# An attention block and a gated feed-forward network on one core: feed-forward chunks of 510 tokens across batches, outputs accumulated in four banks

## Chip, cores and metric

One core of a Trainium2 chip runs the whole kernel. The metric is device microseconds (us) of one execution; lower is better. The engines are PE (matrix products; PEld is its loading of the stationary operand), DVE (VectorE), ACT (ScalarE), POOL (GpSimd) and SP, which issues the DMAs. Tiles have 128 partitions; PSUM, where PE writes, has eight banks of 512 float32 each per partition.

## What is computed

Eight batches, eight heads of 64, 512 local tokens and 32 global ones per batch. Local tokens attend to the 32 global ones and to local ones up to 32 away; global tokens attend to all. The 544 rows of a batch (global first) are the input `x` (512 wide) of a gated network with a convolution of three taps along the tokens of a batch:

```python
out_g = np.matmul(sm(s_g), v_all)                       # 32 global queries, all keys
s_ll = np.where(mask, s_ll, -1000000000.0)              # |i - j| <= 32
out_l = np.matmul(sm(np.concatenate([s_lg, s_ll], axis=-1)), np.concatenate([v_g, v_l], axis=2))
...
h = np.maximum(x @ w_in, 0.0)                           # 512 -> 1024
for k in range(K):                                      # K = 3, zeros at a batch's two ends
    conv_out += conv_w[k][None, None, :] * hp[:, k:k + S, :]
gate = 1.0 / (1.0 + np.exp(-conv_out))
return (h * gate @ w_out).astype(np.float32)            # 1024 -> 512
```

`w_in`, `conv_w` and `w_out` arrive as float64; everything else is float32.

## The kernel before

**Layout.** Features lie on partitions and tokens run along the free dimension. To keep precision, each factor of the two network products is split in a high and a low part of a reduced float32 type, and a product is three matmuls: high by high, high by low, low by high.

**Weights.** Eight packs of 128 × 1024 float64 (four of `w_in`, four of `w_out`) are loaded as pairs of 32-bit words by WD (L171) and decoded: absolute value on ACT (WA, L112), clamp, shift and join of the sign on DVE (WC: L119, L120, L123), the high part cast on ACT (WH, L212), and the low part on DVE from the power of two and the remaining bits (WL: L126, L130, L132, L134). One tile `wt` serves all packs in turn; the raw tiles share their space with the tiles of `g`.

**Attention**, by pair of heads: scores (SC, L264), mask and maximum on DVE (MA, L285), exponentials with their sum on ACT (EX, L295), transposes (TR, L304) copied back by ACT (AT, L212), the product with the values (PV, L325), division (NO, L333), a transpose (UP, L341), then the high part XH (ACT) and the low part XL (DVE, L364) of `x`. The global tokens, four heads at a time, go through G (L278), GM, GE, GT (L406), GC, GP (L422), GO, GQ (L436) and GX, which writes their columns of `x`.

**Network.** A unit is one of 16 half batches (272 tokens) and one of eight feature tiles `ft`. Z (L460) makes twelve matmuls of 274 columns, the half batch and a neighbour on either side, into a bank `ps_h`. RE (L469, ACT) applies the maximum into one of two lasting tiles `hb` whose ends are zero. C1 (L248, POOL) is the middle tap; Ca and Cb (L484, DVE) add the outer ones. For two feature tiles at a time, 544 wide, follow TH (tanh, L493, ACT), GG (the gate times h, L498, DVE), GH (high part, ACT) and GL (low part, L215, on POOL in the first batch, on DVE later). O (L523) is done per half batch and output tile `mt`: two parts Oa and Ob, each of four feature tiles and twelve matmuls of 272 columns, into one bank `ps_o`; OE (L212, DVE) copies it out and ST stores it.

**Order.** `plan` and `units` list all these steps with what they need and which tiles or banks they take. `arranged` simulates them with the costs of `cost` and the limits `SLOTS` and `LIMIT`; among the steps that are ready on an engine, one with the lowest position goes first, and positions come from tables of numbers (`POS0` for the first batch, `POS` for later ones, `WPOS` for weight packs, `LATE`). `emit` issues the steps in that order, and each engine executes its own in exactly that order, whatever is ready.

Of the kernel before, what the change touches and what calls it, by code (L numbers as in the profile page):

```python
# [52 lines left out]
def attn_moe(ctx: ExitStack, tc: tile.TileContext, qk_d, vw_d, qg_d, w_in_d, w_out_d, cw_d, out_d):  # L53
# [61 lines left out]

    def scaled_bits(w1, t, keep):

        v = nc.vector
        v.tensor_scalar(out=f(t), in0=f(t), scalar1=LEAST, scalar2=MOST, op0=ALU.max, op1=ALU.min)  # L119
        v.tensor_scalar(  # L120
            out=t, in0=t, scalar1=3, scalar2=0x3F800000 | keep, op0=ALU.logical_shift_left, op1=ALU.bitwise_and
        )
        v.scalar_tensor_tensor(out=t, in0=w1, scalar=0xC0000000, in1=t, op0=ALU.bitwise_and, op1=ALU.bitwise_or)  # L123
# [4 lines left out]
    def rest(on, out, w0, w1, p, low):  # L128

        nc.vector.tensor_scalar(out=w1, in0=w1, scalar1=low, scalar2=None, op0=ALU.bitwise_and)  # L130
# [1 line left out]
        v.scalar_tensor_tensor(out=f(w1), in0=w0, scalar=2.0**-32, in1=w1, op0=ALU.mult, op1=ALU.add)  # L132
        if on == "v":
            v.scalar_tensor_tensor(out=out, in0=f(w1), scalar=2.0**-20, in1=f(p), op0=ALU.mult, op1=ALU.mult)  # L134
# [210 lines left out]
    def x_of(b, ct, half):  # L345
        if (b, ct, half) not in xs:
            xs[b, ct, half] = (xp.tile([P, HW], F32R, name="xh"), xp.tile([P, HW], F32R, name="xl"))
        return xs[b, ct, half]

    def outputs(n, half):  # L350
# [2 lines left out]
        xh, xl = x_of(b, h // 2, half)
        if half == 0:
            return heads[n]["pv"][:, 0 : HW - SG], xh[:, SG:HW], xl[:, SG:HW]
        return heads[n]["pv"][:, SL - HW : SL], xh, xl

    def XH(n, half):
        pv, xh, xl = outputs(n, half)
        cp("XH", xh, pv)  # L360

    def XL(n, half):
        pv, xh, xl = outputs(n, half)
        nc.vector.tensor_tensor(out=xl, in0=pv, in1=f(xh), op=ALU.subtract)  # L364
# [86 lines left out]
    def Z(u):  # L451
        hh, ft = divmod(u, NFT)
        b, half = divmod(hh, 2)
        st = hid[u] = {"h": hb[u // 2 % SLOTS["hb"]][:, u % 2, half : half + HW]}
        ps = st["z"] = bank([P, HW], "ps_h")
        i = 0
        for ct in range(NCT):
            xh, xl = x_of(b, ct, half)
            for w, x in ((w_in[0], xh), (w_in[0], xl), (w_in[1], xh)):
                nc.tensor.matmul(ps, lhsT=w[:, ft, ct, :], rhs=x, start=i == 0, stop=i == 3 * NCT - 1)  # L460
# [11 lines left out]

    def C1(u):
        st, ft = hid[u], u % NFT
        if u % 2 == 0:
            st["two"] = moe.tile([P, 2, HALF], F32, name="t", bufs=SLOTS["t"])
        else:
            st["two"] = hid[u - 1]["two"]
        st["t"] = st["two"][:, u % 2, :]
# [441 lines left out]
```

## Time and profile before

| | |
|---|---|
| median of three runs | 595.39 us (595.06 to 596.19) |
| profiled execution, device time | 595.32 us |
| its span in the trace | 593.5 us |
| mean granted TensorE clock | 0.982 |
| ACT busy | 324.2 us (55%) |
| DMA | 68.46 MB, mean 115 GB/s |

The page gives busy time by engine over the whole span; the trace is then asked for stretches of time (windows), for the chain of work that ended last, and for groups of like instructions. In 40 slices of 14.8 us the busy tenths of PE and the granted clock are:

```profile
PE   5656997999999999999999999999999999999997
DVE  4999999689477948577685858668584856565651
POOL 6000242033012111121111012111101212221210
PEclk9977999899999999999999999999999999999999
```

The first seven slices differ from all others: PE is half busy there, DVE at nine tenths, POOL free for three of them.

### The profile page before, as it was taken

The numbers are of one execution on the slowest core, as the hardware profiler recorded it, in microseconds if no ns is written. First come the engines' busy times: TensorE is split into PE (matmuls) and PEld (weight loads), VectorE is DVE, ScalarE is ACT, GpSimd is POOL, SyncE is SP. The second block draws the span as 40 slices with busy tenths as digits, with TensorE's granted clock in tenths as the row PEclk, the third lists the DMA queues.
The fourth block names the chain that finished last, engine by engine and source line by source line (L and its number), as shares of the span: only waits on it lengthen the run. The fifth ranks groups of instructions, "written<-read, shape, count | busy, mean of one in ns | idle before, by whom it ended". The sixth has DMA issues, their size and how long they took to land.

```text
span 593.5 us, 20757 instructions
## 1 busy us (share of the span) xinstructions
PE 560.9 (95%) x8704; PEld 528.8 (89%) x8704; DVE 424.0 (71%) x1388; ACT 324.2 (55%) x994; POOL 101.1 (17%) x190
## 2 busy tenths in 40 slices
PE   5656997999999999999999999999999999999997
PEld 3345896999999999999999999999999999999997
DVE  4999999689477948577685858668584856565651
ACT  4954794676477666446565655555565543333320
POOL 6000242033012111121111012111101212221210
PEclk9977999899999999999999999999999999999999
DMA  6987334156234332123333222232412000000001
GB/s 254 390 286 313 95 118 170 39 204 223 91 135 153 107 134 98 56 110 108 135 108 145 100 78 94 100 144 97 146 63 75 20 22 20 29 20 29 30 29 47
DMA packets 22125, 68.46 MB, mean 115 GB/s; under 512 B 2576, under 2 KB 12816, under 8 KB 21008
## 3 DMA queue, kind: packets, MB, share of 16 engines
q1 hardware_dynamic: 22032, 67.14, 31.2%
q8 instruction: 68, 1.11, 0.8%
q14 instruction: 25, 0.20, 0.1%
HBM read 58.22 MB, written 8.91 MB: 113 GB/s over the span
## 4 chain that ended last, share of the span: by engine, by line
PE 84%; DVE 9%; ACT 2%; issue 1%; DMA 1%; POOL 0%; DVEq 0%
PE ps_o L523 32%; PE ps_h L460 31%; PE ps_v L325 5%; PE ps_s L264 4%; PE ps_t L304 4%; PE pv L341 2%; PE psg L278 2%; PE go L422 2%; PE gt L406 1%; DVE pr L285 1%; DVE t L484 1%; DMA vf<-vw 1%; DVE wt L123 1%; DVE raw L132 1%; ACT pr L295 1%
## 5 line engine op out<-in xcount | busy, mean ns | idle before, releaser
L460 PE MATMUL ps_h<-xh,w_in 128*128 128x274 f32 x1024 | 225.4, 298 | 2.8 <-DVE raw L132 1.3
L523 PE MATMUL ps_o<-g,w_out 128*128 128x272 f32 x1536 | 212.2, 290 | 0.0
L523 PEld LDWEIGHTS ps_o<-g,w_out 128*128 128x128 f32 x1536 | 200.0, 189 | 0.2
L460 PEld LDWEIGHTS ps_h<-xh,w_in 128*128 128x128 f32 x1024 | 171.9, 191 | 6.3 <-ACT g L212 1.4
L248 POOL TENSOR_SCALAR t<-hb,cw 128x272 f32<-128x272 f32 x128 | 79.9, 629 | 425.7 <-ACT hb L469 159.2
L460 PE MATMUL ps_h<-xl,w_in 128*128 128x274 f32 x512 | 149.5, 292 | 0.8 <-issue 0.8
L484 DVE SCALAR_TENSOR_TENSOR t<-hb,cw,t 128x272 f32<-128x272 f32 x256 | 125.7, 514 | 30.5 <-POOL t L248 29.1
L295 ACT ACTIVATE pr<-pr,negm 128x128 f32<-128x128 f32 x256 | 99.5, 391 | 47.7 <-DVE negm L285 47.7
L469 ACT ACTIVATE hb<-ps_h 128x273 f32<-128x273 f32 x128 | 50.8, 398 | 93.4 <-PE ps_h L460 91.9
L460 PEld LDWEIGHTS ps_h<-xl,w_in 128*128 128x128 f32 x512 | 98.1, 192 | 1.0 <-issue 1.0
L285 DVE CUSTOM_DVE_ANT_0 pr<-ps_s,mask 128x128 f32<-128x128 f32 x256 | 57.8, 285 | 25.6 <-PE ps_s L264 23.2
L212 DVE COPY o<-ps_o 128x272 f32<-128x272 f32 x64 | 28.0, 438 | 54.8 <-PE ps_o L523 54.6
L212 ACT CAST g<-t 128x544 fp32r<-128x544 f32 x64 | 40.9, 646 | 34.5 <-DVE t L498 22.6
L498 DVE SCALAR_TENSOR_TENSOR t<-t,hb 128x544 f32<-128x544 f32 x64 | 46.0, 719 | 14.3 <-ACT t L493 13.3
L493 ACT ACTIVATE t<-t 128x544 f32<-128x544 f32 x64 | 42.4, 663 | 15.0 <-DVE t L484 13.9
L212 ACT COPY a<-ps_t 128x512 f32<-128x512 f32 x64 | 37.0, 583 | 23.2 <-PE ps_t L304 23.0
L295 ACT ACTIVATION_READ_ACCUMULATOR pr<-pr,negm 128x1 f32 x256 | 48.3, 189 | 0.0
L264 PE MATMUL ps_s<-qk 64*32 64x128 f32 x2048 | 38.4, 283 | 8.4 <-DMA qk<-qk 5.8
L304 PE MATMUL ps_t<-ident,pr 128*128 128x128 f32 x256 | 43.0, 282 | 3.5 <-ACT pr L295 2.5
L215 DVE TENSOR_TENSOR g<-t,g 128x544 fp32r<-128x544 f32 x56 | 41.0, 737 | 6.8 <-ACT g L212 5.3
L264 PEld LDWEIGHTS ps_s<-qk 64*32 64x32 f32 x2048 | 29.9, 109 | 12.7 <-DMA qk<-qk 5.8
L304 PEld LDWEIGHTS ps_t<-ident,pr 128*128 128x128 f32 x256 | 31.1, 144 | 8.2 <-ACT pr L295 7.6
(70 smaller groups left out, 466.1 us busy)
## 6 DMA issues: line engine op xcount, KB each, us to landing
vf<-vw SPq DMA_DIRECT2D x32, 896.0 KB, 6.3
qk<-qk SPq DMA_DIRECT2D x32, 592.0 KB, 4.9
out<-o SPq DMA_DIRECT2D x64, 136.0 KB, 1.7
raw<-w_in SPq DMA_DIRECT2D x4, 1024.0 KB, 6.6
raw<-w_out SPq DMA_DIRECT2D x4, 1024.0 KB, 6.6
qgf<-qg SPq DMA_DIRECT2D x16, 64.0 KB, 2.0
cwr<-cw SPq DMA_DIRECT2D x1, 24.0 KB, 1.9
```

Of the source, the lines that this page charges most:

```text
L212: nc.scalar.copy(out=out, in_=in_) if choice(key) == "a" else eng(key).tensor_copy(out=out, in_=in_)
L248: nc.gpsimd.tensor_scalar(out=out, in0=in_, scalar1=by, scalar2=0.0, op0=ALU.mult, op1=ALU.add)
L264: nc.tensor.matmul(heads[n + j]["s"][b * SG : (b + 1) * SG, t, :], lhsT=qk[rows, i * SG : (i + 1) * SG], rhs=qk[rows, a : a + P], start=Tr ...
L285: nc.vector.tensor_tensor_reduce(out=pr[:, t, :], in0=st["s"][:, t, :], in1=mask[:, t].rearrange("p a c -> p (a c)"), op0=ALU.add, op1=ALU ...
L295: nc.scalar.activation(out=st["p"][:, t, :], in_=st["p"][:, t, :], func=AF.Exp, scale=-1.0, bias=st["m"][:, t : t + 1], accum_out=two["r"] ...
L304: nc.tensor.transpose(out=st["t"][:, t, :], in_=st["p"][:, t, :], identity=ident)
L460: nc.tensor.matmul(ps, lhsT=w[:, ft, ct, :], rhs=x, start=i == 0, stop=i == 3 * NCT - 1)
L469: nc.scalar.activation(out=o, in_=z, func=AF.Relu, scale=0.5)
L484: nc.vector.scalar_tensor_tensor(out=st["t"], in0=st["h"][:, k : k + HALF], scalar=cw[:, 3 * ft + k : 3 * ft + k + 1], in1=st["t"], op0=AL ...
L493: nc.scalar.activation(out=t, in_=t, func=AF.Tanh)
L498: nc.vector.scalar_tensor_tensor(out=t, in0=t, scalar=1.0, in1=h, op0=ALU.add, op1=ALU.mult)
L523: nc.tensor.matmul(ps, lhsT=w[:, mt, ft, :], rhs=g[:, ft, :], start=ft + i == 0, stop=ft == NFT - 1 and i == 2)
```

## The change

**Chunks across batches.** The tokens of all batches form one row: 544 of a batch, then one column of zeros, 4360 columns in all. A chunk is 510 of them; there are eight, and a ninth of 280. Z covers a chunk and a neighbour on either side, 512 columns; the zero columns give the convolution its zeros at a batch's ends. A pair of heads now writes its `x` into two chunks that share the boundary.

**Units.** A unit is a chunk and a feature tile. Z is cut into Za and Zb, six matmuls each. After each unit's gate its share of O follows: Oa (output tiles 0 and 1) and Ob (2 and 3), six matmuls each, added up over the eight feature tiles in four banks that stay taken for the whole chunk. Conv, gate and split are done per unit, 510 wide; `hb` is a fresh tile per unit, and `g` a tile per unit, in four slots that the raw weights share.

**Weights.** Sixteen packs of 512 instead of eight of 1024, by another way: the clamp (L128), the difference of value and high part (WS, L234) and the sum with the remaining bits (WX, L239) are on POOL; DVE keeps two operations for the value (L133, L136) and two for the remaining bits (L139, L227). There are two tiles `wt`.

**Numbers.** All positions are other numbers, `LIMIT` allows one Z bank, four O banks, four attention banks; the output is stored as one row per feature and cut on the host.

```diff
+CW = 510
+ROW = S + 1
...
+    def clamp(e, t):
+        e.tensor_scalar(out=f(t), in0=f(t), scalar1=LEAST, scalar2=MOST, op0=ALU.max, op1=ALU.min)
...
-        t = gp.tile([P, 1024, wpe], WT, name="raw", tag=f"g{i % 2}", padded_shape=[P, NFT * HALF // wpe, wpe])
+        t = gp.tile([P, 512, wpe], WT, name="raw", tag="g", padded_shape=[P, 1024 // wpe, wpe], bufs=SLOTS["g"])
...
+    def WM(i):
+            clamp(nc.gpsimd, wf[i])
...
+            w0, p = raw[i][:, :, 0], raw[i][:, :, 1]
+            power(p, wf[i])
+            nc.vector.scalar_tensor_tensor(
+                out=f(w0), in0=w0, scalar=2.0**-52, in1=f(p), op0=ALU.mult, op1=ALU.mult
+            )
+
+    def WS(i):
+            nc.gpsimd.tensor_tensor(out=lo, in0=f(wf[i]), in1=f(hi), op=ALU.subtract)
+
+    def WX(i):
+            nc.gpsimd.tensor_tensor(out=lo, in0=f(lo), in1=f(raw[i][:, :, 0]), op=ALU.add)
...
-        for ct in range(NCT):
-            xh, xl = x_of(b, ct, half)
-            for w, x in ((w_in[0], xh), (w_in[0], xl), (w_in[1], xh)):
-                nc.tensor.matmul(ps, lhsT=w[:, ft, ct, :], rhs=x, start=i == 0, stop=i == 3 * NCT - 1)
+        ps = hid[u]["z"][:, 0:w]
+        for ct in range(2 * part, 2 * part + 2):
+            x = x_of(c, ct)
+            for i, (k, a) in enumerate(((0, 0), (0, 1), (1, 0))):
+                nc.tensor.matmul(
+                    ps, lhsT=w_in[k][:, ft, ct, :], rhs=x[:, a, 0:w], start=ct + i == 0, stop=ct == NCT - 1 and i == 2
+                )
...
-        for ft in range(part * 4, part * 4 + 4):
-            for i, (w, g) in enumerate(((w_out[0], gh), (w_out[1], gh), (w_out[0], gl))):
+        for mt in range(2 * part, 2 * part + 2):
+            o = NCT * c + mt
+            if ft == 0:
+                ops[o] = bank([P, CW], "ps_o")
+            for i, (k, a) in enumerate(((0, 0), (1, 0), (0, 1))):
                 nc.tensor.matmul(
-                    ps, lhsT=w[:, mt, ft, :], rhs=g[:, ft, :], start=ft + i == 0, stop=ft == NFT - 1 and i == 2
+                    ops[o][:, 0:w], lhsT=w_out[k][:, ft, mt, :], rhs=gs[u][:, a, 0:w], start=ft + i == 0,
+                    stop=ft == NFT - 1 and i == 2,
                 )
...
-LIMIT = dict(h=2, o=2, at=5)
+LIMIT = dict(h=1, o=4, at=4)
...
+WPOS = [16.39, -20.62, -19.23, -4.18, 58.21, 58.89, 45.08, 86.23, 4.32, 33.55, 14.23, 33.92, 0.44, 73.48, -12.53, -0.0]
```

The planned order moves at three places. First PE in the middle of the program, where one batch's attention meets the network. Before, a score group (L264), a value product (L325) and a global score (L278) stand singly between whole Z's and O parts:

```order
L460 MATMUL ps_h<-xh,w_in_152 128x274
L264 MATMUL ps_s<-qk 32x128 x32
L325 MATMUL ps_v<-vf,a 32x64 x32
L278 MATMUL psg_3526<-qk,qgf 32x480 x4
L278 MATMUL psg_3527<-qk,qgf 32x64 x4
L460 MATMUL ps_h<-xh,w_in_151 128x274
```

After, at a batch's start (scores L294, global scores L308, transposes L334, Z L499):

```order
L294 MATMUL ps_s<-qk 32x128 x64
L499 MATMUL ps_h<-x,w_in_153 128x512 x2
L499 MATMUL ps_h<-x,w_in_154 128x512
L499 MATMUL ps_h<-x,w_in_153 128x512 x2
L499 MATMUL ps_h<-x,w_in_154 128x512
L308 MATMUL psg_5807<-qk,qgf 32x480 x4
L308 MATMUL psg_5808<-qk,qgf 32x64 x4
L334 MATMUL ps_t<-ident,pr 128x128 x4
L499 MATMUL ps_h<-x,w_in_153 128x512 x2
L499 MATMUL ps_h<-x,w_in_154 128x512
```

Two score groups now go together, half a Z stands between attention steps, and the narrow transposes follow at once.

The second place is ACT at the same point of the changed program (exponentials L325, copies L242, the maximum of Z L509):

```order
L325 ACTIVATE pr,sums<-pr,negm 128x128 x4
L509 ACTIVATE hb<-ps_h 128x512
L325 ACTIVATE pr,sums<-pr,negm 128x128 x4
L420 ACTIVATE pg,gsum<-pg,gnegm 128x544
L242 COPY a<-ps_t 128x512
L325 ACTIVATE pr,sums<-pr,negm 128x128 x4
```

The exponentials of a batch's heads follow each other with little of the network between them.

The third place is the start of POOL and DVE. On POOL, before, nothing stands between the set-up of the mask and the first middle taps:

```order
L103 MEMSET mask 32x32
L105 COPY mask<-corner 32x32
L248 TENSOR_SCALAR t<-hb_155,cw 128x272 x2
L248 TENSOR_SCALAR t<-hb_156,cw 128x272 x2
L215 TENSOR_TENSOR g_1240<-t,g_1239 128x544
```

After, the weights' operations stand there (clamp L128, difference L234, sum L239):

```order
L116 COPY mask<-corner 32x32
L128 TENSOR_SCALAR wt<-wt 128x512
L234 TENSOR_TENSOR w_in_154<-wt,w_in_153 128x512
L128 TENSOR_SCALAR wt<-wt 128x512
L239 TENSOR_TENSOR w_in_154<-w_in_154,raw 128x512
L128 TENSOR_SCALAR wt<-wt 128x512
L234 TENSOR_TENSOR w_in_154<-wt,w_in_153 128x512
L239 TENSOR_TENSOR w_in_154<-w_in_154,raw 128x512
```

On DVE the first mask (L315) now has a weight pack ahead of it, which takes what POOL has clamped:

```order
L172 TENSOR_TENSOR cw<-cw,cwp 128x24
L133 TENSOR_SCALAR wt<-wt 128x512
L136 SCALAR_TENSOR_TENSOR wt<-raw,wt 128x512
L315 ISA pr,negm<-ps_s,mask 128x128
L315 ISA negm 128x1
```

Before, the first mask (L285) came right behind the convolution weights' last operation. The packs come in the order 1, 2, 14, 3, 15, 12, 8, 10, 0, 9, 11, 6, 4, 5, 13, 7 (0 to 7 are `w_in` by feature tile, 8 to 15 `w_out`).

More of the change, by code (lines that the diff above doesn't have):

```diff
@@ L143, in attn_moe @@
     WT = F32 if wpe == 1 else U32
+    zeros = const.tile([P, 2, 2], F32, name="zeros")
+    nc.vector.memset(zeros, 0.0)
     def drop(t):
@@ L343, in UP, with x_of, outputs, XH @@
             )
[L345 to L350, printed above, removed]
-        b, h = divmod(n, H)
[L353 to L364, printed above, removed]
+    def x_of(c, ct):
+        if (c, ct) not in xs:
+            xs[c, ct] = xp.tile([P, 2, CW + 2], F32R, name="x")
+        return xs[c, ct]
+    def outputs(n, part):
+        b, h = divmod(n, H)
+        m = first_part(b)
+        x = x_of(b + part, h // 2)
+        if part == 0:
+            return heads[n]["pv"][:, 0:m], x[:, :, CW + 2 - m :]
+        return heads[n]["pv"][:, m - 2 :], x[:, :, 0 : SL + 2 - m]
+    def XH(n, part):
+        pv, x = outputs(n, part)
+        cp("XH", x[:, 0], pv)
+    def XL(n, part):
+        pv, x = outputs(n, part)
+        nc.vector.tensor_tensor(out=x[:, 1], in0=pv, in1=f(x)[:, 0], op=ALU.subtract)
+        b, h = divmod(n, H)
+        if part == 1 or b == 0:
+            c = SL + 2 - first_part(b) if part == 1 else 0
+            k = 2 if b == B - 1 else 1
+            nc.vector.tensor_copy(out=x_of(b + part, h // 2)[:, :, c : c + k], in_=zeros[:, :, 0:k])
     def GM(n):
@@ L471, in RE, with tap @@
             nc.vector.tensor_scalar(out=o, in0=z, scalar1=0.0, scalar2=0.5, op0=ALU.max, op1=ALU.mult)
+    def tap(u, k):
+        c, ft = divmod(u, NFT)
+        w = width(c, B)
+        return hid[u]["t"][:, 0:w], hid[u]["h"][:, k : k + w], cw[:, 3 * ft + k : 3 * ft + k + 1]
     def C1(u):
[L474 to L479, printed above, removed]
@@ L491, in TH @@
     def TH(u):
-        t = hid[u]["two"]
+        t, h, w = tap(u, 1)
         nc.scalar.activation(out=t, in_=t, func=AF.Tanh)
     def GG(u):
-        t, half = hid[u]["two"], u // NFT % 2
-        h = hb[u // 2 % SLOTS["hb"]][:, :, half + 1 : half + 1 + HALF]
+        t, h, w = tap(u, 1)
         nc.vector.scalar_tensor_tensor(out=t, in0=t, scalar=1.0, in1=h, op0=ALU.add, op1=ALU.mult)
     def GH(u):
-        hh, ft = divmod(u, NFT)
-        if hh not in gs:
-            gs[hh] = [gp.tile([P, NFT, HALF], F32R, name=f"g{i}") for i in range(2)]
@@ L653, in plan, with op @@
     N, ops, at, held = B * H, [], {}, set()
-    def op(key, i, pos, later, before=(), takes=(), uses=()):
+    def op(key, i, pos, later, before=(), takes=(), uses=(), n=CW):
         same = "XH" if key == "YH" else key
@@ L658, in op @@
         if names:
-            e = dict(p=PE, s=SP, a=ACT)[names[0]]
-            c = "v"
+            e = dict(p=PE, v=DVE, g=POOL, s=SP, a=ACT)[names[0]]
+            c = WAY[i] if key in ("WL", "WC") else "v"
         else:
```

298 lines of the change are left out of this document (157 added, 141 removed).

## The prediction

> **What bounds the kernel now.** I read the page's busy times first, then its chain of work by engine and line.
>
> ```profile
> PE 560.9 (95%) x8704; PEld 528.8 (89%) x8704; DVE 424.0 (71%) x1388; ACT 324.2 (55%) x994; POOL 101.1 (17%) x190
> ...
> PE 84%; DVE 9%; ACT 2%; issue 1%; DMA 1%; POOL 0%; DVEq 0%
> PE ps_o L523 32%; PE ps_h L460 31%; PE ps_v L325 5%; PE ps_s L264 4%; PE ps_t L304 4%; PE pv L341 2%; PE psg L278 2%; PE go L422 2%; PE gt L406 1%; DVE pr L285 1%; DVE t L484 1%; DMA vf<-vw 1%; DVE wt L123 1%; DVE raw L132 1%; ACT pr L295 1%
> ```
>
> PE is 95% busy and holds 84% of the chain; 63% is the FFN's two products (Z at L460, O at L523). Windows show where it is not the bound.
>
> ```profile
> core 0: us, PE busy (x) PEld busy (x) DVE busy (x) ACT busy (x) POOL busy (x), PEclk, DMA share, GB/s
> 5.00:111.00 106.00, 83.14 (x1697) 69.15 (x1698) 93.58 (x306) 69.39 (x218) 19.91 (x48) 0.90 0.59 222
> 30.00:45.00 15.00, 8.22 (x236) 7.45 (x226) 14.62 (x30) 8.75 (x26) 0.00 (x0) 0.73 0.81 291
> 300.00:500.00 200.00, 199.21 (x3093) 191.08 (x3082) 139.12 (x469) 110.94 (x348) 30.14 (x47) 1.00 0.25 89
> ```
>
> Two stages, then. Up to about 111 us DVE sets the pace (14.62 of 15 us) with the weights' decoding, the first batches' attention and the first gates, while PE stands and POOL is free. From there on PE misses 0.8 us in 200. So I count PE work for the second stage, and for the first how long PE stands.
>
> **The FFN's matmuls: −33.8 us.** The chain gives the paces at full clock.
>
> ```profile
> 301.40 1.72 PE ps_h L460 x12
> ...
> 308.96 1.52 PE ps_h L460 x12
> ...
> 569.28 21.06 PE ps_o L523 x168
> ```
>
> O: 21.06 / 168 = 125.4 ns for 272 columns. Z: 1.52 / 12 = 127 ns for 274. Before has 128 × 12 = 1536 of each: 192.6 + 195.0 = 387.6 us. After has 64 full units and 8 short ones of 12 + 12: 768 of 512 columns, 768 of 510, 192 of 282 or 280. The columns streamed hardly change (838,656 before; 838,848 after); only the count falls, 3072 to 1728. So the term depends on how much of the 125 ns is not streaming. A stretch at half clock tells:
>
> ```profile
> 105.43 0.43 PE L460 MATMUL ps_h<-xl,w_in 128*128 128x274 f32 x1
> ...
> 106.58 0.66 PE L523 MATMUL ps_o<-g,w_out 128*128 128x272 f32 x2
> 105.20:108.20 3.00, 3.00 (x15) 3.00 (x15) 0.37 (x1) 1.39 (x2) 0.49 (x1) 0.50 0.01 3
> ```
>
> Five matmuls of 274 start from 105.43 up to the O at 106.58: 230 ns each at a granted clock of 0.50. Twice the clock would make that 115 ns, or 0.42 ns a column; at full clock 127 is seen, 12 ns more. Something that doesn't scale with the clock takes over. The next rows say what is likely.
>
> ```profile
> L523 PEld LDWEIGHTS ps_o<-g,w_out 128*128 128x128 f32 x1536 | 200.0, 189 | 0.2
> L304 PE MATMUL ps_t<-ident,pr 128*128 128x128 f32 x256 | 43.0, 282 | 3.5 <-ACT pr L295 2.5
> L304 PEld LDWEIGHTS ps_t<-ident,pr 128*128 128x128 f32 x256 | 31.1, 144 | 8.2 <-ACT pr L295 7.6
> 288.67 0.60 PE L304 MATMUL ps_t<-ident,pr 128*128 128x128 f32 x4
> ```
>
> Before each matmul a new weight tile is loaded, recorded at 189 ns, longer than the 125 ns of pace: the loads are pipelined, yet PEld is busy 89% of the span. I read 125 to 127 ns as the pace of the loads at 272 columns, which a stream of 512 × 0.42 = 215 ns would hide. The four transposes support that weakly: each loads 128 columns, records 144 ns, and paces at about 107 ns ((600 − 282 of the last) / 3, a single one being recorded at 282), so a load can go faster than 125 ns when less streams. Then after costs 768 × 0.215 + 768 × 0.214 + 192 × 0.126 (short ones still at the load's pace) = 353.8 us, −33.8. The other end: the 12 ns stay with each matmul, and only 1536 rather than 3072 of them count: 768 × 0.227 + 768 × 0.226 + 192 × 0.130 = 372.9, −14.7. I take −33.8, because the half-clock row shows the 12 ns gone where the stream takes 230 ns, which is the nearest row to 215.
>
> The Trainium skill (TensorE: Matmul & The Clock Gate, Back-to-back issue gap) puts one isolated matmul of 512 at N/2.4 + 2.5, some 216 ns, and a sustained stream of load and matmul pairs at about 131 ns. The first agrees with the 0.42 ns a column here; the second is a rival below.
>
> What attention costs PE, and how long PE stands at the start, follows from windows of single lines from 110.9 us to the last matmul, L460, L523 and L304 in this order:
>
> ```profile
> 110.90:590.40 479.50, 201.85 (x1392) 183.19 (x1392) 1.00 0.26 92
> 110.90:590.40 479.50, 201.57 (x1466) 189.78 (x1464) 1.00 0.26 92
> 110.90:590.40 479.50, 28.99 (x192) 22.67 (x192) 1.00 0.26 92
> ```
>
> 1392 × 0.127 + 1466 × 0.1254 = 360.6 us of FFN; 192 of the 256 transposes are six batches; 479.5 − 360.6 − 2 of small waits leaves 117 us, 19.5 a batch. So by 110.9 PE had done two batches (39) and 144 + 70 FFN matmuls (27), and had stood, or lost to the lower clock, **45 us**.
>
> **More changes of mode: +5 us.** Attention matmuls use parts of the array (32 or 64 rows). Z behind such a group takes 1.72 us, elsewhere 1.52 (301.40 against 308.96): 0.2 us per group. By the instruction order PE goes into such groups 42 times before and 66 after: 24 × 0.2 = 4.8. Bounds 0 (the price was already there per matmul) to 7.
>
> **Attention in bursts: +7.5 us.** Before spreads a batch's attention among sixteen Z's and O's. After issues, for the last five batches, the scores of two of its four pairs of heads together, then all other steps of local attention among three or four Z's, then mostly FFN. In that burst ACT carries by the order 8 heads of exponentials, 8 evictions, 5 Z evictions, 3 tanh, 5 casts of x, 2 of g and the global part.
>
> ```profile
> L295 ACT ACTIVATE pr<-pr,negm 128x128 f32<-128x128 f32 x256 | 99.5, 391 | 47.7 <-DVE negm L285 47.7
> L212 ACT COPY a<-ps_t 128x512 f32<-128x512 f32 x64 | 37.0, 583 | 23.2 <-PE ps_t L304 23.0
> L469 ACT ACTIVATE hb<-ps_h 128x273 f32<-128x273 f32 x128 | 50.8, 398 | 93.4 <-PE ps_h L460 91.9
> ```
>
> That is 32 × 0.391 = 12.5, 8 × 0.583 = 4.7, 5 × 0.6 (512 for 273 columns, from 398 ns) = 3.0, and about 6.8 for the rest, 27 us, behind a lead of some 2 us until the first scores are masked. PE's own work there: 19.5 less about 2 of a global group issued later, and four Z's of 2.58 (12 × 0.215), 28. So ACT's 29 against PE's 28: a wait of about 1 us, 1.5 taken since the order is fixed, five times, 7.5. Bounds 0 (the Z's cover it) and 3 us each, 15. Between bursts FFN fills PE and neither has much to do (DVE 139, ACT 111 of 200 us in the window).
>
> **The start: −3 us.** What moves: per pack, DVE loses clamp, subtraction and half of the low part.
>
> ```profile
> L123 DVE SCALAR_TENSOR_TENSOR wt<-raw,wt 128x1024 uint32<-128x1024 uint32 x8 | 10.8, 1354 | 0.3
> L132 DVE SCALAR_TENSOR_TENSOR raw<-raw 128x1024 f32<-128x1024 uint32 x8 | 10.1, 1261 | 0.3
> L120 DVE TENSOR_SCALAR wt<-wt 128x1024 uint32<-128x1024 uint32 x8 | 5.7, 716 | 0.3
> L130 DVE TENSOR_SCALAR raw<-raw 128x1024 uint32<-128x1024 uint32 x8 | 5.6, 694 | 0.0
> L126 DVE TENSOR_SCALAR wt<-wt 128x1024 uint32<-128x1024 uint32 x8 | 5.5, 685 | 0.0
> L119 DVE TENSOR_SCALAR wt<-wt 128x1024 f32<-128x1024 f32 x8 | 5.4, 674 | 0.2 <-ACT wt L112 0.2
> L134 DVE SCALAR_TENSOR_TENSOR w_out<-raw,wt 128x1024 fp32r<-128x1024 f32 x4 | 5.1, 1268 | 0.1
> L134 DVE SCALAR_TENSOR_TENSOR w_in<-raw,wt 128x1024 fp32r<-128x1024 f32 x4 | 4.9, 1226 | 0.1
> ```
>
> 53.1 us on DVE become the same forms of L120, L123, L126 and L132, twice as many at half the size: 32.1 us and a little more for twice the fixed part, say 35. −18 us on the engine that binds. But POOL gets per pack a clamp and two operations with two inputs. No row has them; the nearest:
>
> ```profile
> 76.77 0.49 POOL L248 TENSOR_SCALAR t<-hb,cw 128x272 f32<-128x272 f32 x1
> 77.22 1.36 POOL L215 TENSOR_TENSOR g<-t,g 128x544 fp32r<-128x544 f32 x1
> 541.04 1.36 DVE L215 TENSOR_TENSOR g<-t,g 128x544 fp32r<-128x544 f32 x2
> 541.86 2.02 POOL L248 TENSOR_SCALAR t<-hb,cw 128x272 f32<-128x272 f32 x3 [7.89 <-DVE g L215]
> 542.79 2.19 DVE L484 SCALAR_TENSOR_TENSOR t<-hb,cw,t 128x272 f32<-128x272 f32 x4 [0.39 <-POOL t L248]
> ```
>
> One input, 512 columns: between 0.49 and 0.49 × 512/272 = 0.92, 0.75 taken. Two inputs: 1.36 × 512/544 = 1.29. 16 × (0.75 + 2 × 1.29) = 53 us on POOL, if DVE leaves it alone. It doesn't: the three at 541.86 take 2.02 instead of 1.47, the first of them beside the end of DVE's two-input subtraction.
>
> The Trainium skill (SBUF — State Buffer, Who interferes with whom) has VectorE and GpSimd share a pair of ports with an exclusive lock; it speaks against this move, and the 2.02 against 1.47 agrees. It would make the 53 us longer by whatever DVE holds.
>
> The order also puts the first pack's decode ahead of the first mask on DVE, waiting for a clamp that POOL can only begin after the mask's set-up.
>
> ```profile
> 11.01 0.21 POOL L105 COPY mask<-corner 32x32 f32<-32x32 f32 x1
> 7.97 0.29 DVE L285 CUSTOM_DVE_ANT_0 pr<-ps_s,mask 128x128 f32<-128x128 f32 x1 [3.37 <-PE ps_s L264]
> ```
>
> So the first mask moves from 7.97 to about 12 (11.2 + 0.75): 4 us, with all of the first batch's exponentials behind it. And pack 0, which the first Z needs, is ninth in the order.
>
> ```profile
> 53.57 0.37 PE L460 MATMUL ps_h<-xh,w_in 128*128 128x274 f32 x1
> 80.48 0.75 PE L523 MATMUL ps_o<-g,w_out 128*128 128x272 f32 x4
> ```
>
> Walking the new order with these prices, the first Z comes at 57 to 63 (before 53.57) and the first O at about 80 (80.48), and chunk 0's last g between 115 and 133; PE has then stood 35 to 48 us, middle 42 against 45: −3. Bounds −15 (most of DVE's 18 us come through) and +10 (POOL at twice its price in the stretch that counts).
>
> **Elsewhere nothing.** Wider operations on DVE and ACT after the start, the copies of zeros between batches and the larger stores are hidden: DVE has 61 and ACT 89 free us in the 200 of the window. The last unit's short g (280 columns) is ready about 4.2 us after its Z, with 4.6 us of O still queued, so the tail stays.
>
> **Sum**, against the profiled run: span 593.5 − 33.8 + 4.8 + 7.5 − 3 = 569.0, and 1.8 us lie outside the span (595.32 measured), so **571**. The median of the runs shown is 595.39, the same. About 0.2%, 1.2 us, is what a measurement can tell from no change.
>
> **Rivals.**
> - *The 12 ns stay with each matmul.* For it: no row has a wider stream with a load at full clock, and a fixed turn-round per matmul could look like the 12 ns. Against: half clock shows none of it. Price 19.1 us: 590.
> - *POOL becomes the bound of the start* (the slower side). 48 operations and eight or so of chunk 0's own; if each waits for DVE and takes 3.0 us on average, the packs end at 11 + 144 = 155, not at about 122. The last packs feed chunk 0's last Z and O; until these run its four accumulators stay taken, chunk 1's O can't begin, and the four g tiles fill. PE stands 33 us longer: 604. Slower than before it becomes when the packs end 24 us later than I take, at an average above 2.8 us. For it: 14.6 of 15 us of DVE busy. Against: DVE has 18 us less to do.
> - *The start gains its bound of 15 us and the bursts cost nothing:* 571 − 12 − 7.5 = 551.5.
> - *A wide matmul takes as long as a narrow one:* 125 to 127 ns would be a floor of each pair of load and matmul, whatever streams. 1728 × 0.127 = 219 us of FFN, 436 in all. The 230 ns at half clock, in proportion to the clock for all but 12 ns, speaks against it. The 131 ns of the Trainium skill (TensorE: Matmul & The Clock Gate, Back-to-back issue gap) would come out near it.
>
> That the change doesn't do what it says is excluded: the order has 1728 such matmuls.
>
> **Numbers.** Forecast 0.58 (own range 557 to 587: start and bursts at their bounds, not all at once), the 12 ns 0.22 (577 to 603), POOL 0.10, both gains 0.09, the far figure 0.01. With 0.2 to be left out, POOL's 0.10 goes, the top of the 12 ns, the far figure and half of the fourth: range **553 to 597**. Slower: POOL's 0.10 and what of the 12 ns lies over 596.6, 0.14; same 0.04; faster 0.82.
>
> **What would show it.** The chain's runs of twelve O's at 2.57 us (214 ns) say the load is hidden; 2.71 says the 12 ns stay. Windows of the start: DVE no longer at 14.6 of 15, the first Z after 57, chunk 0's last POOL operation on packs before 133. PE idle before ps_t and ps_v, released by ACT, should sum to about 8 us after 130. I am wrong if POOL is busy without a break beyond 140, or if the granted clock falls below the 1.00 of 300 to 500 when the matmuls grow longer, which nothing here shows.

## The result, and the profile after

The changed kernel takes 624.20 us (median of 4, 623.72 to 626.43), the kernel before 595.79 beside it (median of 4, 595.06 to 597.51): a ratio of 1.048, 95% interval 1.0445 to 1.0515. It is slower by 4.8%, where 571 was forecast. The profiled execution has a span of 621.9 us, 28.4 more than before. Its page, busy times and the chain by engine and line:

```profile
PE 571.5 (92%) x7360; PEld 451.3 (73%) x7360; DVE 417.6 (67%) x1305; ACT 323.5 (52%) x970; POOL 149.4 (24%) x182
...
PE 78%; DVE 13%; issue 4%; POOL 2%; ACT 2%; DMA 1%; SPq 0%; POOLq 0%; ACTq 0%; DVEq 0%
PE ps_o L556 29%; PE ps_h L499 28%; PE ps_v L355 4%; PE ps_s L294 4%; PE ps_t L334 4%; DVE raw L227 2%; PE pv L371 2%; PE psg L308 2%; DVE pr L315 1%; PE go L460 1%; DVE wt L136 1%; DVE wt L133 1%; DVE raw L139 1%; PE gt L444 1%; DVE t L525 1%
```

PE has 1344 matmuls less and is busy longer. The two products still hold 57% of a longer chain, 354 us where they held 63%, 374; DVE's share rose from 9 to 13%, and POOL, which was not on the chain, is. The chain inside the network shows the pace (start, length, engine, tile and line, count):

```profile
320.72 1.41 PE ps_h L499 x6
322.13 1.41 PE ps_o L556 x6
323.54 1.40 PE ps_h L499 x6
324.94 1.40 PE ps_o L556 x6
...
337.54 1.05 PE psg L308 x16
338.59 1.58 PE ps_o L556 x6
...
349.04 2.03 PE ps_s L294 x124
351.07 1.59 PE ps_h L499 x6
```

Six take 1.40 us, 233.5 ns each, not 215; behind a narrow group six take 1.58. Near the end, the timeline has both widths:

```profile
581.50 0.93 PE L499 MATMUL ps_h<-x,w_in 128*128 128x282 f32 x6
582.26 1.54 PE L556 MATMUL ps_o<-g,w_out 128*128 128x510 f32 x6
583.65 0.95 PE L499 MATMUL ps_h<-x,w_in 128*128 128x282 f32 x6
584.43 1.56 PE L556 MATMUL ps_o<-g,w_out 128*128 128x510 f32 x6
```

From 581.50 to 582.26 and from 583.65 to 584.43, six of 282 take 0.76 and 0.78 us: 127 to 130 ns each. With the 125.4 ns of 272 before, all three lie on one line, 2.5 + 0.452 ns a column. As the columns streamed are as many after as before, so is the time.

The windows of the stretches that matter (columns as in the prediction), first of the kernel before, then of the changed one:

```profile
15.00:60.00 45.00, 29.09 (x650) 21.02 (x646) 43.67 (x116) 30.45 (x92) 1.05 (x1) 0.82 0.84 324
60.00:111.00 51.00, 46.18 (x837) 42.60 (x837) 45.38 (x154) 34.39 (x109) 13.36 (x16) 0.96 0.33 115
160.00:500.00 340.00, 338.43 (x5373) 323.59 (x5372) 240.50 (x830) 194.32 (x612) 51.96 (x83) 1.00 0.29 101
```

```profile
15.00:60.00 45.00, 32.60 (x740) 23.34 (x745) 43.21 (x152) 33.82 (x121) 31.08 (x20) 0.85 0.68 236
60.00:111.00 51.00, 41.94 (x707) 30.29 (x690) 49.38 (x147) 34.91 (x109) 42.24 (x28) 0.87 0.47 159
111.00:160.00 49.00, 45.65 (x499) 35.19 (x498) 36.63 (x92) 24.06 (x68) 21.53 (x17) 0.97 0.19 63
160.00:500.00 340.00, 329.72 (x4531) 259.95 (x4530) 212.90 (x751) 182.83 (x570) 28.70 (x41) 1.00 0.32 112
```

Until 111 us DVE is no emptier than it was (43.2 of 45 us against 43.7, 49.4 of 51 against 45.4), and POOL is full now too (42 of 51). From 160 to 500 PE is idle for 10.3 of 340 us, where before it was for 1.6.

To see where the 28.4 us came from, PE's work is counted at fixed prices in every kernel: a network matmul at 2.5 + 0.452 ns a column, attention at one price per step (17.2 us a batch, near the shortest groups seen). What a stretch holds beyond that is called lost: standing, half clock, changes of mode.

```
                    work    lost by 160   160 to 500   500 to end    span
before              524.3       51.6         14.0          3.6       593.5
after               521.0       67.3         28.4          5.2       621.9
difference           -3.3      +15.7        +14.4         +1.6       +28.4
```

The wide matmuls brought 3.3 us instead of 33.8, the start cost 15.7 instead of gaining 3, and the middle lost 14.4 where 12.3 had been forecast (4.8 + 7.5).

### The profile page after: what moved, and what is told of

Read it like the earlier page. It is cut to its first block, busy times and chain, and to the rows that moved or that the text cites. A ratio compares the mean times of both kernels' runs of the same rounds, so it can differ in the third digit from the quotient of the medians.

```text
span 621.9 us, 17936 instructions
## 1 busy us (share of the span) xinstructions
PE 571.5 (92%) x7360; PEld 451.3 (73%) x7360; DVE 417.6 (67%) x1305; ACT 323.5 (52%) x970; POOL 149.4 (24%) x182
## 4 chain that ended last, share of the span: by engine, by line
PE 78%; DVE 13%; issue 4%; POOL 2%; ACT 2%; DMA 1%; SPq 0%; POOLq 0%; ACTq 0%; DVEq 0%
PE ps_o L556 29%; PE ps_h L499 28%; PE ps_v L355 4%; PE ps_s L294 4%; PE ps_t L334 4%; DVE raw L227 2%; PE pv L371 2%; PE psg L308 2%; DVE pr L315 1%; PE go L460 1%; DVE wt L136 1%; DVE wt L133 1%; DVE raw L139 1%; PE gt L444 1%; DVE t L525 1%
## 5 line engine op out<-in xcount | busy, mean ns | idle before, releaser
L499 PE MATMUL ps_h<-x,w_in 128*128 128x512 f32 (+1 forms) x864 | 220.5, 390 | 1.4 <-issue 1.4
L556 PE MATMUL ps_o<-g,w_out 128*128 128x510 f32 (+1 forms) x864 | 217.4, 390 | 0.4 <-POOL g L245 0.4
L499 PEld LDWEIGHTS ps_h<-x,w_in 128*128 128x128 f32 x864 | 154.9, 189 | 35.5 <-issue 3.1
L556 PEld LDWEIGHTS ps_o<-g,w_out 128*128 128x128 f32 x864 | 153.5, 189 | 32.0 <-POOL g L245 0.8
L278 POOL TENSOR_SCALAR t<-hb,cw 128x510 f32<-128x510 f32 (+1 forms) x72 | 51.4, 713 | 420.0 <-ACT hb L509 354.1
L525 DVE SCALAR_TENSOR_TENSOR t<-hb,cw,t 128x510 f32<-128x510 f32 (+1 forms) x144 | 106.6, 741 | 55.1 <-POOL t L278 53.9
L325 ACT ACTIVATE pr<-pr,negm 128x128 f32<-128x128 f32 x256 | 99.6, 395 | 36.5 <-DVE negm L315 36.3
L529 ACT ACTIVATE t<-t 128x510 f32<-128x510 f32 (+1 forms) x72 | 43.9, 610 | 72.8 <-DVE t L525 69.4
L509 ACT ACTIVATE hb<-ps_h 128x512 f32<-128x512 f32 (+1 forms) x72 | 41.5, 576 | 54.4 <-PE ps_h L499 53.5
L533 DVE SCALAR_TENSOR_TENSOR t<-t,hb 128x510 f32<-128x510 f32 (+1 forms) x72 | 48.3, 676 | 25.1 <-ACT t L529 25.1
L242 ACT CAST g<-t 128x510 fp32r<-128x510 f32 (+1 forms) x72 | 42.9, 597 | 39.6 <-PE ps_o L556 20.7
L315 DVE CUSTOM_DVE_ANT_0 pr<-ps_s,mask 128x128 f32<-128x128 f32 x256 | 56.6, 285 | 9.0 <-PE ps_s L294 8.8
L245 DVE TENSOR_TENSOR g<-t,g 128x510 fp32r<-128x510 f32 (+1 forms) x64 | 42.0, 658 | 24.5 <-ACT g L242 24.3
L334 PE MATMUL ps_t<-ident,pr 128*128 128x128 f32 x256 | 46.7, 299 | 10.3 <-ACT pr L325 8.9
L294 PE MATMUL ps_s<-qk 64*32 64x128 f32 x2048 | 40.0, 288 | 13.5 <-DMA qk<-qk 9.0
L325 ACT ACTIVATION_READ_ACCUMULATOR pr<-pr,negm 128x1 f32 x256 | 49.2, 192 | 0.0
L334 PEld LDWEIGHTS ps_t<-ident,pr 128*128 128x128 f32 x256 | 32.8, 149 | 22.5 <-ACT pr L325 12.8
L294 PEld LDWEIGHTS ps_s<-qk 64*32 64x32 f32 x2048 | 31.4, 111 | 20.1 <-DMA qk<-qk 9.0
L242 ACT COPY a<-ps_t 128x512 f32<-128x512 f32 x64 | 35.8, 582 | 13.8 <-PE ps_t L334 13.7
L242 ACT CAST x<-pv 128x479 fp32r<-128x479 f32 (+7 forms) x64 | 23.1, 373 | 37.6 <-PE pv L371 23.5
L355 PE MATMUL ps_v<-vf,a 128*32 128x64 f32 x2048 | 37.8, 226 | 5.1 <-issue 5.1
```

The lines of the kernel that those rows point to most:

```text
L242: nc.scalar.copy(out=out, in_=in_) if choice(key) == "a" else eng(key).tensor_copy(out=out, in_=in_)
L278: nc.gpsimd.tensor_scalar(out=out, in0=in_, scalar1=by, scalar2=0.0, op0=ALU.mult, op1=ALU.add)
L294: nc.tensor.matmul(heads[n + j]["s"][b * SG : (b + 1) * SG, t, :], lhsT=qk[rows, i * SG : (i + 1) * SG], rhs=qk[rows, a : a + P], start=Tr ...
L315: nc.vector.tensor_tensor_reduce(out=pr[:, t, :], in0=st["s"][:, t, :], in1=mask[:, t].rearrange("p a c -> p (a c)"), op0=ALU.add, op1=ALU ...
L325: nc.scalar.activation(out=st["p"][:, t, :], in_=st["p"][:, t, :], func=AF.Exp, scale=-1.0, bias=st["m"][:, t : t + 1], accum_out=two["r"] ...
L334: nc.tensor.transpose(out=st["t"][:, t, :], in_=st["p"][:, t, :], identity=ident)
```

## Experiments

**The pace by itself.** Streams of matmuls with nothing beside them, four weight tiles in turn. The main loop, and the POOL operations:

```diff
+    for i in range(96):
+        o, s, e = slot(i)
+        nc.tensor.matmul(o, lhsT=wr[:, i % 4, :], rhs=xr[:, :], start=s, stop=e)
...
+        nc.gpsimd.tensor_scalar(out=u, in0=d[0], scalar1=LEAST, scalar2=MOST, op0=ALU.max, op1=ALU.min)
+        nc.gpsimd.tensor_scalar(out=u, in0=d[0], scalar1=c, scalar2=0.0, op0=ALU.mult, op1=ALU.add)
```

> Streams of 96 matmuls by themselves, each with its own weight load, in place of the whole kernel (nothing of the reference is computed): reduced float32 of 512, 512, 272, 128 columns with four weight tiles in turn, 512 of zeros, bfloat16 of 512 and 272, 512 with one weight tile, 400; beside them, four each on POOL: clamp (max, min), multiply by a column and add, multiply and add of numbers, max alone, add of two tiles. In the changed kernel 512 columns take 233.5 ns, 282 take 130, 272 took 125.4 before: 2.5 + 0.452 a column. Theory A (the stream of reduced float32 itself goes at 0.452 ns a column at full clock): 512 takes 234, 272 takes 125, also alone, 128 about 60 or the load's floor; bfloat16 512 at most 217. Theory B (other engines' traffic slows it in the kernel): alone, 512 takes about 216 and 272 about 116. Theory C (the clock is really lower than granted, for all work): bfloat16 512 takes 234 too. Theory D (it hangs on the data): zeros take 216, the rest 234. The clamp on POOL: 1.9 us if it is the two operations with numbers that cost, 0.7 as the multiply by a column if it was only contention in the kernel.

Groups by line and shape (busy time of 96, mean of one):

```profile
L116 PE MATMUL ps<-xr,wr 128*128 128x512 f32 x96 | 21.9, 389 | 0.0
L128 PE MATMUL ps<-xb,wb 128*128 128x512 bf16 x96 | 20.9, 379 | 0.0
L137 PE MATMUL ps<-xr,wr 128*128 128x400 f32 x96 | 17.5, 341 | 0.0
L119 PE MATMUL ps<-xr,wr 128*128 128x272 f32 x96 | 12.2, 288 | 0.0
L131 PE MATMUL ps<-xb,wb 128*128 128x272 bf16 x96 | 11.3, 279 | 0.0
L122 PE MATMUL ps<-xr,wr 128*128 128x128 f32 x96 | 10.8, 275 | 0.0
L154 POOL TENSOR_SCALAR u<-d 128x512 f32<-128x512 f32 x4 | 7.8, 1945 | 4.2 <-DVE d L90 4.0
L162 POOL TENSOR_TENSOR u<-d,d 128x512 f32<-128x512 f32 x4 | 5.2, 1290 | 0.3
L156 POOL TENSOR_SCALAR u<-d,c 128x512 f32<-128x512 f32 x4 | 2.8, 698 | 0.4
```

A mean holds the overlap with the next one; the pace is the busy time over 96, less a little for the last one's end. From start to start it is 227 ns for 512, 180 for 400, 125.3 for 272, 111 for 128; in bfloat16 216 and 116. The two bfloat16 widths differ by 0.417 ns a column (100 ns for 240). At that rate 2.5 ns are left over in bfloat16, and 12 to 14 ns in reduced float32. So the 12 ns are there without a load coming late (in the stream of 128 columns a load and its matmul come every 111 ns, under the 113 that 272 columns stream at 0.417), without traffic, and with zeros as data too (22.0 us for 96). Theory A has it, but for the 6.5 ns by which 512 in the kernel exceeds 227. And the clamp, a `max` and a `min` by numbers, takes 1.95 us on POOL where the multiplication of the same tile by a column takes 0.70.

**Does the tile or the kernel make the 6.5 ns?** Streams with the kernel's weight tiles and pitches, and a third run with more widths:

```diff
+        nc.tensor.matmul(o[:, 0:512], lhsT=w_in[v // 2][:, k, ct, :], rhs=xa[ct][:, v % 2, 0:512], start=s, stop=e)
...
+        nc.tensor.matmul(o[:, 0:512], lhsT=w_in[0][:, 0, 0, :], rhs=xb[0][:, 0, 0:512], start=s, stop=e)
+        nc.tensor.matmul(o[:, 0:512], lhsT=w_in[0][:, k, ct, :], rhs=xa[0][:, 0, 0:512], start=s, stop=e)
```

> Streams of 96 matmuls alone again (nothing of the reference is computed). Alone, with one moving tile, 512 columns took 227 ns (one pass of 512 at 0.417 a column, 213.3, and 13.7); in the changed kernel they take 231, 232 and 237 in a fixed pattern by which of high and low part moves. Stages, 512 columns unless said: one moving tile twice (warm, then counted); weights and moving tiles as in Z with the kernel's pitch of 514; the same with pitch 512; weights high and low with one moving tile; one set of weights with moving tiles at pitch 512; at pitch 514; two halves of one tile; 510 columns as in O; 274 as in Z before; 256. Theory A (the pitch or start of the moving tile costs): pitch 514 about 233, pitch 512 227. Theory B (changing the moving tile costs, at any pitch): all stages with changing tiles 231 to 237, one tile 227. Theory C (changing between high and low weights): only stages with both weights over 227. Theory D (traffic of the other engines in the kernel): all stages 227. The 274 columns: 127 as in the kernel before.

> Streams alone once more (nothing of the reference is computed), reduced float32, for what is still open in the pace: 512 columns took 227 ns with four weight tiles in one small tile, 232 to 233 with 32 of them in the kernel's large one. Stages of 96: 32 weight tiles; four of them; one; four of the other large tile with another moving tile; 32 with another moving tile; 480, 448, 384 and 320 columns with 32. Then six times 32 narrow matmuls (float32, 64 rows, 32 by 128) and 12 wide ones, and 256 narrow ones in a row. Theory A (it is which weights are loaded): four tiles or one 227, 32 tiles 232. Theory B (where the moving tile lies): all stages on one moving tile alike. Widths: 12 to 13 ns above 0.417 a column up to 400; if 448 and 480 keep 12 and 13, the rise to 19 is 512's own. Narrow: a wide group behind a narrow one about 0.2 us longer, as 1.59 against 1.40 in the changed kernel; if PE waits for its own instructions in long narrow runs, the 256 in a row show breaks of 0.8 to 1.5 us, each behind a 16 KB transfer on the instruction queue, although no other transfer runs.

In the first of the two every stage of 512 or 510 columns went at 232 to 233 ns, with one moving tile or many, at a pitch (columns from one part of a tile to the next) of 514 or 512; 274 took 127.1 and 256 118.7. All four theories of that run, as they were put, fall: it is neither pitch nor change of tile nor traffic. The third run's groups:

```profile
L113 PE MATMUL ps<-xb,w_in 128*128 128x512 f32 x96 | 22.5, 395 | 0.0
L118 PE MATMUL ps<-xb,w_in 128*128 128x512 f32 x96 | 22.5, 395 | 0.0
L123 PE MATMUL ps<-xa,w_in 128*128 128x512 f32 x96 | 22.6, 395 | 0.0
L128 PE MATMUL ps<-xa,w_in 128*128 128x512 f32 x96 | 22.0, 389 | 0.0
L133 PE MATMUL ps<-xb,w_in 128*128 128x480 f32 x96 | 21.1, 379 | 0.0
L138 PE MATMUL ps<-xb,w_in 128*128 128x448 f32 x96 | 19.7, 366 | 0.0
```

With `xb[0]` as the moving tile, four weight tiles (L113) or one (L118) make no difference (232 ns). With `xa[0]` and 32 weight tiles (L128) it is 227, where `xb[0]` with these 32 took 232 too, and the two tiles hold the same numbers: what is left is where the moving tile lies. With `xa[3]` and other weights (L123) it is 233. For the tile `xb[0]` the excess over 0.417 a column grows from 13 ns at 320 (146.6) through 16 at 384 (176.0) and 18 at 480 (217.8) to 19 at 512. Why a place costs this stays open. The same run put 12 wide matmuls behind 64 narrow records (a float32 matmul leaves two) six times: 2.98 us from the first wide one to the next group, against 12 × 0.232 = 2.78. The 0.2 us for a change of mode holds alone. A row of 512 narrow records went without a break.

**The parts in bfloat16, in both kernels.** The parts have eight bits instead of the longer ones, so the products are less exact; order and counts are kept. Elsewhere only what the type asks for follows: views and padding of tiles and, in the kernel before, two masks of the decoding.

```diff
-F32R = mybir.dt.float32r
+F32R = mybir.dt.bfloat16
```

> The changed kernel with the parts of x, g and the weights in bfloat16 instead of reduced float32 (eight bits a part, so the products are less exact), order and counts kept. Alone, bfloat16 took 216 ns for 512 and 116 for 272 columns, where reduced float32 took 227 to 233 and 125 to 127. Theory 1 (what each matmul costs above its stream belongs to reduced float32, not to the load of the weights being late or to the kernel's traffic): in the kernel 512 columns take 216 instead of 233.5, 1536 x 17.5 = 27 us and 2 us for the short ones, of which the start's share (about 15%) is hidden: 597 to 600. Rival (the kernel's traffic costs it): 229 or more a matmul, 617 to 624.

> The kernel before, its order kept, with the same parts in bfloat16. Theory 1: 125.4 and 127 ns become 116 and 116.5, 3072 x 9.9 = 30 us less, 28 of it behind the start: 567. If narrow matmuls were held by the load of the weights instead (my prediction's reading), the bfloat16 load, 98 ns against 188, would also free them, but then the wide ones in the changed kernel would gain nothing. Rival: DVE, ACT or the start binds before PE does, 580 or more.

The changed kernel falls to 589.55 us (588.04 to 592.28; 0.991 of the kernel before, interval 0.9875 to 0.9941), the kernel before to 562.04 (561.13 to 564.32; 0.945, interval 0.9416 to 0.9487). The first one's timeline and the second one's chain:

```profile
501.37 1.46 PE L499 MATMUL ps_h<-x,w_in 128*128 128x512 bf16 x6
502.66 1.45 PE L556 MATMUL ps_o<-g,w_out 128*128 128x510 bf16 x6
```

```profile
535.37 1.40 PE ps_h L460 x12
536.77 19.47 PE ps_o L523 x168
```

215 ns for 512 columns (501.37 to 502.66, by six; 216 on average over the trace), 115.9 for 272 (19.47 / 168): the paces of the bare streams. At 0.417 instead of 0.452 ns for each of some 838,700 columns, PE's work falls by 29 us in either kernel, and the wide kernel is still the slower by 27.5. The excess belongs to reduced float32 and is there at either width; width as such buys next to nothing even in bfloat16 (0.422 a column against 0.426). Both gains came out above what was expected (34.7 and 32.8 us), so some 3 to 5 us of lost time went too.

The traces also show when the excess is absent. While the granted clock is 0.50, wide matmuls start 427 ns apart in the changed kernel (three in a row from 105.07 to 106.35 us) and 427 apart in its bfloat16 form too: 0.83 ns a column, with no excess in either type.

**The clamp back on DVE; then all the weights' work.** One word in the first, three in the second; the order of everything else is kept.

```diff
-            clamp(nc.gpsimd, wf[i])
+            clamp(nc.vector, wf[i])
...
-            nc.gpsimd.tensor_tensor(out=lo, in0=f(wf[i]), in1=f(hi), op=ALU.subtract)
+            nc.vector.tensor_tensor(out=lo, in0=f(wf[i]), in1=f(hi), op=ALU.subtract)
...
-            nc.gpsimd.tensor_tensor(out=lo, in0=f(lo), in1=f(raw[i][:, :, 0]), op=ALU.add)
+            nc.vector.tensor_tensor(out=lo, in0=f(lo), in1=f(raw[i][:, :, 0]), op=ALU.add)
```

> The changed kernel, its order kept, with only the clamp of the sixteen packs done by DVE instead of POOL. In the changed kernel the clamp takes 2.05 us on POOL, 33 us in all, and DVE's own four weight operations took 52 us though they take about 33 where POOL rests. Theory 1 (the clamp's length on POOL, and what it holds up on DVE, is most of the longer start): DVE takes 16 x 0.34 = 5.4 us more and its four operations some 8 less, the chain from first pack to first mask shortens by 1.5 us, the start loses 8 to 12 us less: 612 to 616. Rival (the order of the packs and their chain sets the start, not the clamp): within 3 of 624.

> The changed kernel, its order kept, with all three POOL operations of the weights (clamp, difference, sum) on DVE. DVE gets 16 x (0.34 + 0.69 + 0.69) = 27.5 us, and its other weight operations fall from 52 to about 33. Theory 1 (POOL's length and its hold on DVE cost the start): DVE's weights come to 60 us, 8 more than now, but no step waits for POOL and the start's other operations are not stretched: 612 to 624. Rival (DVE alone is the bound, POOL's help was real): slower than 624 by 8 or more, 632.

The clamp alone: 619.48 us (617.39 to 621.30). Everything on DVE: 613.92 (612.78 to 615.12). What the engines paid in the changed kernel, by group:

```profile
L128 POOL TENSOR_SCALAR wt<-wt 128x512 f32<-128x512 f32 x16 | 32.8, 2053 | 8.8 <-ACT wt L123 8.7
L227 DVE SCALAR_TENSOR_TENSOR raw<-raw 128x512 f32<-128x512 uint32 x16 | 17.0, 1062 | 0.5
L136 DVE SCALAR_TENSOR_TENSOR wt<-raw,wt 128x512 uint32<-128x512 uint32 x16 | 14.2, 884 | 0.6
L139 DVE TENSOR_SCALAR raw<-wt 128x512 uint32<-128x512 uint32 x16 | 11.0, 685 | 0.0
L133 DVE TENSOR_SCALAR wt<-wt 128x512 uint32<-128x512 uint32 x16 | 9.8, 614 | 9.0 <-POOL wt L128 9.0
L402 DVE CAST x<-zeros 128x2 fp32r<-128x2 f32 x32 | 10.6, 333 | 0.0
```

And the same work with POOL at rest:

```profile
L136 DVE SCALAR_TENSOR_TENSOR wt<-raw,wt 128x512 uint32<-128x512 uint32 x16 | 12.1, 757 | 0.6
L227 DVE SCALAR_TENSOR_TENSOR raw<-raw 128x512 f32<-128x512 uint32 x16 | 11.5, 719 | 0.5
L133 DVE TENSOR_SCALAR wt<-wt 128x512 uint32<-128x512 uint32 x16 | 7.5, 471 | 0.0
L139 DVE TENSOR_SCALAR raw<-wt 128x512 uint32<-128x512 uint32 x16 | 6.7, 418 | 0.0
L402 DVE CAST x<-zeros 128x2 fp32r<-128x2 f32 x32 | 6.0, 186 | 0.0
```

DVE's four operations take 52.0 us beside a busy POOL and 37.8 beside an idle one. The change had moved 78 us of work to POOL and left DVE with the 53 us of before. With all on DVE it pays 67 us and the kernel is 10 us faster. The clamp alone gave 5 us, half of what theory 1 said, while the other two steps stayed on POOL and DVE's four operations still took 49 us.

**The former decoding, newly planned.**

```diff
-WAY = "qqqqqqqqqqqqqqqq"
+WAY = "vvvvvvvvvvvvvvvv"
```

> The changed kernel with every pack decoded wholly on DVE by the former way (its own branch in the code), newly planned with the same positions. Theory 1 (the decoding by POOL is why the start lost 67 us instead of 52): the start comes near the former one, 609 to 614. Rival (the start is longer by the new chunks and positions): 620 to 630.

632.80 us (631.43 to 635.15), slower than either theory said. The positions were numbers for other steps; the planner put packs ahead of attention, the first batch's `x` was complete at 88 us in place of 61, and 74.2 us were lost by 160. A part undone together with a new plan says nothing about the part. The next run keeps the changed decoding, all of it on DVE, and searches for positions that fit it.

**All positions anew.** The planner knows that the weights are on DVE, has the prices of the trace, and its tables of positions are searched again:

```diff
-    p=("S", "G", "T", "GT", "P", "U", "GP", "GQ", "Za", "Zb", "Oa", "Ob"), v=("WL", "WC"), g=("WS", "WT", "WM"), s=("LQ", "LV", "LG", "WD", "ST"),
+    p=("S", "G", "T", "GT", "P", "U", "GP", "GQ", "Za", "Zb", "Oa", "Ob"), v=("WL", "WC", "WS", "WT", "WM"), s=("LQ", "LV", "LG", "WD", "ST"),
...
-        return 11 + n * 5 // 12
+        return 14 + n * 43 // 100
```

> The changed kernel with all weights' work on DVE, known to the planner, its costs corrected by the trace (512 columns 234 ns, DVE's operations with two tiles held up beside POOL), and all positions searched anew. Theory 1 (what is left of the longer start in the run with the weights on DVE, 60.5 us lost by 160 against 51.6 before, and half of the bursts' 14 us, come from the positions): 600 to 608. Rival (they come from chunks of all four x tiles being needed before the first Z and from DVE's larger load): 612 to 618.

608.34 us (606.27 to 610.29), just above the 600 to 608 of theory 1. The counts of all these kernels, and in the last two columns, from 160 to 500, PE's pauses of over 0.15 us and how often it goes into a narrow group:

```
                    lost by 160   160 to 500   500 to end   first Z   pauses   narrow groups
before                  51.6         14.0         3.6         53.6      1.6          22
after                   67.3         28.4         5.2         76.3     10.3          41
clamp on DVE            64.1         25.5         5.0         73.1
weights on DVE          60.5         25.6         4.7         72.3      8.0          40
replanned               54.1         26.7         4.5         52.8      3.9          58
```

Step by step the runs take back 13.2 of the start's 15.7 us: 3.2 with the clamp, 3.6 with the rest of POOL's share, 6.4 with the positions; 2.5 are left. All positions changed at once, so no single one is shown to cost the 6.4. A likely one is that of pack 0, ninth in the changed kernel: it was complete at 72.8 us, and the first Z came at 76.3, though its first two `x` tiles were ready at 49. In the middle, lost less pauses is 12.4, 18.1, 17.6 and 22.8 for 22, 41, 40 and 58 groups: a straight line of 0.29 us a group above 6.0. The new plan halved the pauses and paid for it in groups.

**Both causes together.**

> The same with the weights' clamp, difference and sum on DVE (613.9 us with reduced float32). Theory 1 (the two causes add): 613.9 - 25 = 589. Rival (with PE quicker, DVE's start or the bursts bind and take the gain back): 600 or more.

584.74 us (582.64 to 586.89; 0.983 of before, interval 0.9779 to 0.9871): 29.2 less than with reduced float32. The rival is out; the two causes add for the most part: singly they gave 34.7 and 10.3 us, together 39.5. The fastest of all kernels is the one before with bfloat16 parts, at the price of shorter parts.

## Why the prediction was wrong

- **The wide matmuls: the step that failed.** The prediction said: "I read 125 to 127 ns as the pace of the loads at 272 columns, which a stream of 512 × 0.42 = 215 ns would hide". The longer stream hid nothing: 227 to 233.5 ns were seen. The excess is no wait for a load, which can come every 111 ns: it comes with each reduced float32 matmul, 12 ns at 272 and 13 to 20 at 512, by which moving tile it is. The rival of 12 ns had the kind right (0.22) and 590 as its time; as the excess grew with the width, even its −14.7 us became −3.3. The half-clock row that decided between the two misled: at half clock the excess was gone at 272, which was read as "the 12 ns gone where the stream takes 230 ns". It shows only that the excess is hidden at half the rate of columns: at 512 it is gone there too (427 ns), while the 213 ns that 512 columns stream at full clock do not hide it. And the transposes, 106 ns for 128 columns, were read as loads that go faster when less streams; the bare stream of 128 columns agrees (111 ns), and so spoke against a wait for loads at 125. The Trainium skill (TensorE: Matmul & The Clock Gate, Back-to-back issue gap) has 216 ns for a single matmul of 512 and 131 for a stream of them. Bfloat16 streams here at the first figure, and nothing came near the second.
- **The start: the sign was wrong.** −3 was forecast, with bounds of −15 and +10; it was +15.7. Three terms were mis-sized. The clamp on POOL was put at 0.75 us from a multiplication; it takes 1.95 alone and 2.05 here, 21 us more over sixteen packs. And DVE was given 35 us for its four operations; they took 52, so the "−18 us on the engine that binds" was −1. The 2.02 against 1.47 had been seen, yet sharing was charged to POOL alone, and not to DVE. (The Trainium skill, SBUF — State Buffer, Who interferes with whom, has the lock shut out either engine; the 52.0 against 37.8 agrees.) The first mask came at 14.26 (forecast 12), the first Z at 76.3 (57 to 63), the first O at 109.3 (80), chunk 0's last pack at 134.6 (122). A late first mask alone is not what counts: in the replanned kernel it came at 18.26, and the first Z at 52.8. The third was the walk through the order: with POOL's share taken out the first Z still came at 72.3, and only with other positions at 52.8, so the order itself cost more than 57 to 63 allowed for.
- **The slower rival** had the place (POOL at the start) and a chance of 0.10. Its trigger, packs ending beyond 146, was not reached; alone the start's error of 18.7 us would have made 571 into 590, not slower than before. It took the missing gain of the matmuls.
- **Changes of mode and bursts** were right in sum, for the bursts by luck: 12.3 forecast, 14.4 measured, 5.7 of it for 19 more narrow groups and 8.7 in pauses. The 7.5 were forecast as waits for ACT, and behind 145 us the trace has no wait of PE for ACT; the pauses are put down to no releaser (last section).
- **The tail:** +1.0 us forecast as nothing. From the last matmul's end it is 4.2 us to the end (617.7 to 621.9) against 3.2: the last of four banks are copied out behind one another, 0.46 each, and a copy waits for a store ahead of it.

## What to carry to other kernels

Before counting matmuls, plot the pace against the width: where two or three widths lie on a line through nearly zero, fewer and wider ones buy nothing, and the type of the operands may be the lever (33 to 35 us here). When work is moved to an engine that shares a port with the binding one, price the moved operation itself, not a like one, and charge its time to both. Undo one part in a fixed order first; a new plan around it answers another question.

## What the runs showed that was not expected

Reduced float32 costs 9 to 17 ns more a matmul than bfloat16, and some 6 ns of it at 512 columns (227 or 233) hang on where the moving tile lies, with nothing else running. Whether a part of the rest belongs to the loads is open: every stream here has a load for each matmul, recorded at 188 ns in reduced float32 and 98 in bfloat16, and none was run without. What grows with the width and changes with the moving tile can't be the load alone.

PE's pauses in the bursts are put down to no releaser:

```profile
369.13 0.76 PE L355 MATMUL ps_v<-vf,a 128*32 128x64 f32 x38
370.97 0.63 PE L355 MATMUL ps_v<-vf,a 128*32 128x64 f32 x26 [1.09 <-issue]
```

```profile
437.32 0.64 PE L355 MATMUL ps_v<-vf,a 128*32 128x64 f32 x29
439.18 0.75 PE L355 MATMUL ps_v<-vf,a 128*32 128x64 f32 x35 [1.22 <-issue]
```

Most come in the middle of a narrow group, and each of the seven over 0.8 us has a 16 KB transfer of the instruction queue starting 0.8 to 1.5 us ahead of it, of 58 such in 622 us. The five such pauses with the weights on DVE and the three of the replanned kernel lie behind one in the same way, by 0.8 to 1.6 us. PE may wait there for its next instructions, which bursts use up fastest. That is not shown: alone, 512 narrow records in a row, slower ones at 27 ns each against 17 here, went through four such transfers without a break.
